# The last difference and low parts of x on VectorE instead of GpSimd, and part of w_out's preparation moved into the last stage

## The chip, the cores and the metric

The kernel runs on one core of a Trainium2 chip. The metric is the device time of one execution in microseconds (us); the time of a kernel is the median of its runs. Engines are called TensorE (PE in the profile; PEld is its loading of weights), VectorE (DVE), ScalarE (ACT), GpSimd (POOL) and SyncE (SP, which only issues DMAs here).

## What is computed

The reference is a chain of three parts in float32:

- attention within chunks of 64 tokens: 8 batches, 8 heads, 576 tokens, head size 64; softmax of q k^T / 8 and the product with v. Its output is a matrix x of 4608 tokens by 512;
- a mixture of 8 experts with capacity 576: the pairs of token and expert are taken in order of falling logit, so that each token gets one expert and each expert 576 tokens; each token's row then goes through relu(x @ w1[e]) @ w2[e], with 1024 hidden values;
- a last feed-forward part:

```python
def _moe2_ref(x, w1, w2, w3, w_out):
    h = np.maximum(np.maximum(x @ w1, x @ w2), x @ w3)   # 512 -> 768
    return (h @ w_out).astype(np.float32)                # 768 -> 512
```

## The kernel before, in words

Attention, routing and the experts come first (to about 656 us of the span). Products are made from float32 numbers that are split into a high part, which TensorE reads as float32r, and a low part, the rest. A split is two operations: ScalarE makes the high part by a cast, then another engine subtracts it from the number, which gives the low part.

The **last stage** is the third part of the reference. It runs over 6 blocks of 768 tokens (`for s in range(NS)`, line 1353). A 2x2 block product is done with seven products (a scheme of Strassen's kind): x of a block comes as four quarters b11, b12, b21, b22, and sums of them are needed, t1 = b12 - b11, t2 = b22 - t1, t3 = b22 - b12, t4 = b21 - t2. `xsum` (line 1070) makes one of these differences, `xsplit` (line 1077) splits one operand into high and low. Unsplit t1 and t4 share one place in the tile `hm`, t2 and t3 the other.

In a block, k runs over nine groups of columns of w1, w2 and w3. Each group has seven products, `p1` to `p7` (lines 1250 to 1281), of six matmuls each (line 1215). `p1` writes the PSUM bank px from b11, and ScalarE copies px to a row of the tile `tmp` (line 1254, its U1). `p6` writes py from t2, and VectorE adds U1 to it (line 1260, U2). `p2` accumulates b21's product onto the same px, so it has to follow the copy. `p5` (t1) writes pz, and `p7` (t3) accumulates onto py, so it has to follow line 1260. `p4` (t4) and `p3` (b22) belong to the group before: of the first group (k = 0) they come at k = 1. So k = 0 has the five products p1, p6, p2, p5, p7, in that order. Each product takes one of 8 tiles of weights (`ws`), and asks for the one 8 products on by a DMA on SP's queue (`wload`, line 1029).

When the nine groups of a block are done, h (unsplit in HR, split in HB) is multiplied with w_out for three sets of tokens, t = 3s, 3s + 1, 3s + 2: again seven products each (`o1` to `o7`, line 1294), with VectorE's sums `c22`, `c21`, `c12` (lines 1338 to 1351), and two scatters each of rows of the result by GpSimd (`scatter`, line 1304). Two sets are interleaved; then GpSimd drains (`pool.drain()`, line 1445) and the third set follows.

Between these products the kernel prepares the next block's x, where `more` is true (5 of the 6 blocks): t1, b11, t2, t4, b21 with VectorE's subtractions, and at the very end t3's difference and the low parts of t3, t4 and b22 with GpSimd's (lines 1456, 1460, 1461, 1469).

`wout(q, what)` (line 1036) prepares a third of w_out: "load" issues its DMAs, "sums" makes four differences on GpSimd, and `wout(q, range(...))` splits its seven operands, with ScalarE's casts (line 1063) and GpSimd's subtractions (line 1064). Thirds 1 and 2 are prepared in the first block of the last stage (lines 1376 to 1389). Third 0 is prepared in the last expert's second layer, `for d in range(4)` (lines 1177 to 1195), beside the preparation of the first block's x; its differences lie in `FP["u"]`, the tile whose first part is the `tmp` of the last stage.

The order of work on each engine is the order in which the program emits it (`tc.manual_schedule()`); an engine takes its instructions in that order, and the waits between engines come from the data. Nothing reorders the code around the change.

```python
    def xsplit(o, eng):
        nc.scalar.copy(XO[o][:, 0], xraw(o))
        eng.tensor_tensor(XO[o][:, 1], xraw(o), XO[o][:, 0].bitcast(F32), op=OP.subtract)
```

Of the kernel before, what the change touches and what calls it, by code (L numbers as in the profile page):

```python
# [7 lines left out]
F32 = mybir.dt.float32  # L8
# [691 lines left out]
def kernel(ctx, tc, q, k, v, w_gate, w1, w2, m1, m2, m3, m_out, out, mark=lambda n: None):  # L700
# [9 lines left out]
    rt = Router(ctx, tc, mark)  # L710
# [5 lines left out]
    P = rt.W = ctx.enter_context(tc.tile_pool(name="mw", bufs=1))  # L716
# [257 lines left out]

    split()
    XO, XR, WS, FP = {}, {}, [], {}
    HB, WQ, HR = {}, {}, {}
    USES = []
    for g in range(9 * NS):
        USES += [(g, 1), (g, 0)] + [(g - 1, 3), (g - 1, 6)] * (g % 9 > 0) + [(g, 2), (g, 4), (g, 5)]  # L980
# [2 lines left out]
    def homes():  # L983

        for o in ("b11", "t3", "b21", "b22", "t1", "t2", "t4"):
            XR[o] = ring.tile([128, 2048], F32R, name="x" + o, tag="chunk")
            XO[o] = XR[o][:, :4 * TB].rearrange("p (c a t) -> p c a t", c=2, a=2)
        W0 = [P.tile([128, 7, 256], F32R, name="wo%d" % i, tag=t) for i, t in enumerate(("c64", "pair"))]
        W1 = [ring.tile([128, 2048], F32R, name="wq%d" % i, tag="chunk")[:, :1792].rearrange("p (n f) -> p n f", n=7)
              for i in range(2)]  # L990
        WQ[0], WQ[1] = W0, W1
        for n, o in enumerate(("b11", "b21", "b22", "t1", "t2", "t3", "t4")):
            for x in range(2):
                WQ[0, n, x], WQ[1, n, x] = W0[x][:, n], W1[x][:, n]
                WQ[2, n, x] = XR[o][:, 4 * TB + 256 * x:4 * TB + 256 * x + 256]
        for i in range(2):
            t = P.tile([128, 4, 2, 2, 128], F32R, name="ws%d" % i, tag="raw%d" % i)
            WS.extend(t[:, j] for j in range(4))
        FP["u"] = P.tile([128, 5 * DM], F32, name="tmp", tag="xg")
        FP["m"] = ring.tile([128, 2048], F32, name="hm", tag="chunk")  # L1000
        FP["x"] = P.tile([128, 4 * TB], F32, name="xt", tag="aoh")

# [23 lines left out]
    def raw(x):  # L1026
        return x[:, 1].bitcast(F32)
# [8 lines left out]
    def wout(q, what):  # L1036

        mark("wout")
        lo = [WQ[q, n, 1].bitcast(F32) for n in range(7)]
        if what == "load":  # L1040
            top, low = mo[256 * q:256 * q + 128, :], mo[256 * q + 128:256 * q + 256, :]
            if q < 2:
                t = WQ[q][1].bitcast(F32)
                nc.sync.dma_start(t[:, 0:6:5], top.rearrange("p (c f) -> p c f", c=2))
                nc.sync.dma_start(t[:, 1:3], low.rearrange("p (c f) -> p c f", c=2))
            else:
                for n, (r, c) in ((0, (top, 0)), (5, (top, 256)), (1, (low, 0)), (2, (low, 256))):
                    nc.sync.dma_start(lo[n], r[:, c:c + 256])
        elif what == "sums":
            tq = WQ["t", q] = [FP["u"][:, 256 * i:256 * i + 256] if q == 0 else  # L1050
                               OT[2 * q - 2 + i // 2][:, i % 2 * 256:i % 2 * 256 + 256] for i in range(4)]
            for to, x, y in ((tq[0], lo[5], lo[0]), (tq[1], lo[2], tq[0]), (tq[3], lo[1], tq[1]), (tq[2], lo[2], lo[5])):
                nc.gpsimd.tensor_tensor(to, x, y, op=OP.subtract)
        else:
            jobs = [(WQ[q, n, 0], WQ[q, n, 1], lo[n] if n < 3 else WQ["t", q][n - 3]) for n in what]
            if q < 2 and what[0] == 0:
                jobs = [(WQ[q][0][:, 0:3], WQ[q][1][:, 0:3], WQ[q][1][:, 0:3].bitcast(F32))]
            elif q < 2:
                jobs = [(WQ[q][0][:, n:n + 2], WQ[q][1][:, n:n + 2],
                         (FP["u"][:, 256 * (n - 3):256 * (n - 1)] if q == 0 else OT[2 * q - 2 + (n - 3) // 2])  # L1060
                         .rearrange("p (n f) -> p n f", n=2)) for n in (3, 5)]
            for hi, to, x in jobs:
                nc.scalar.copy(hi, x)
                nc.gpsimd.tensor_tensor(to, x, hi.bitcast(F32), op=OP.subtract)
# [5 lines left out]
    def xsum(o, eng):  # L1070
        mark("ysplit")
        b12 = raw(XO["t3"])
        a, b = {"t1": (b12, xraw("b11")), "t2": (xraw("b22"), xraw("t1")), "t3": (xraw("b22"), b12),
                "t4": (xraw("b21"), xraw("t2"))}[o]
        eng.tensor_tensor(xraw(o), a, b, op=OP.subtract)

    def xsplit(o, eng):
        mark("ysplit")
        nc.scalar.copy(XO[o][:, 0], xraw(o))
        eng.tensor_tensor(XO[o][:, 1], xraw(o), XO[o][:, 0].bitcast(F32), op=OP.subtract)  # L1080
# [9 lines left out]
    for r in range(E):  # L1090
# [54 lines left out]
        if r + 1 == E:  # L1145
# [8 lines left out]
            dve, pool = nc.vector, nc.gpsimd  # L1154
        state["l1"] = False
        for d in range(4):
            have(8 * r + 4 + d + 1)
            w = [x.rearrange("p (a f) -> p a f", a=8) for x in chunks[8 * r + 4 + d]]
            acc = PS.tile([128, 2, 512], F32, name="acc")
            for hf in range(2):  # L1160
                tk = slice(hf * 288, hf * 288 + 288)
                n = 0
                for f in range(8):
                    mark("mm2")
                    for a, x in ((0, hh), (1, hh), (0, hl)):
                        nc.tensor.matmul(acc[:, hf, :288], w[a][:, f, :], x[:, f, tk], start=n == 0, stop=n == 23)  # L1166
                        n += 1
                    if n % 6 == 0 and n < 24:
                        pump()
                if hf == 1:  # L1170
                    mark("yev")
                    ys = P.tile([128, CAP], F32, name="ys", bufs=2)
                    nc.scalar.copy(ys.rearrange("p (a t) -> p a t", a=2), acc[:, :, :288])  # L1173
                    nc.scalar.dma_start(yd[d * 128:d * 128 + 128, r * CAP:(r + 1) * CAP], ys)
                    state["used"] += 1
                pump()
            if r + 1 == E:
                if d == 0:
                    xsum("t1", dve)
                    xsplit("b11", dve)  # L1180
                    xsum("t2", dve)
                    xsplit("t1", dve)
                elif d == 1:
                    xsum("t4", dve)
                    xsplit("t2", dve)
                    xsplit("b21", dve)
                    wout(0, "sums")
                elif d == 2:
                    xsum("t3", dve)
                    xsplit("t3", dve)  # L1190
                    xsplit("t4", dve)
                    wout(0, range(3))
                else:
                    xsplit("b22", dve)
                    wout(0, range(3, 7))


    c3.close()
# [1 line left out]
    blocks()  # L1200
    TMP = FP["u"][:, :5 * TB].rearrange("p (n t) -> p n t", n=5)
    OT = [P.tile([128, 512], F32, name="ot", tag="ys", bufs=2) for _ in range(2)]
    OT += [P.tile([128, 512], F32, name="ot2", tag="ct"), rt.C.tile([128, 512], F32, name="ot3", tag="i32")]
    XB, YZ, U = {}, {}, {}
    tt = dve.tensor_tensor
    scat = []
# [146 lines left out]
    for s in range(NS):  # L1353
        for k in range(9):
            g, q = 9 * s + k, (k - 1) // 3
            p1(g)
            p6(g)
            if k:
                p4(g - 1)
                if k % 3 == 0:  # L1360
                    hsum(q, dve, "s1", "s2", "s3")
                    high(q, "s1", "s3", "s2")
                    low(q, pool, "s1")
                p3(g - 1)
                if k % 3 == 0:
                    hsum(q, pool, "s4")
                    high(q, "a12", "s4")
                    low(q, pool, "s3", "a12", "s2", "a22", "a11", "s4")
            p2(g)
            if k % 3 == 2:  # L1370
                high(k // 3, "a22")
            p5(g)
            p7(g)
            if k % 3 == 2:
                high(k // 3, "a11")
            if s == 0:
                if k == 0:
                    wout(1, "load")
                elif k == 1:
                    wout(1, "sums")  # L1380
                    wout(1, range(3))
                elif k == 2:
                    wout(1, range(3, 7))
                    wout(2, "load")
                elif k == 4:
                    wout(2, "sums")
                    wout(2, range(3))
                elif k == 5:
                    wout(2, range(3, 7))
        more = s + 1 < NS  # L1390
        t = 3 * s
# [61 lines left out]
        o7(t)  # L1453
        if more:
            xsplit("b21", dve)
            xsum("t3", pool)
        o5(t)
        c22(t)
        if more:
            xsplit("t3", pool)  # L1460
            xsplit("t4", pool)
        o4(t)
        c21(t)
        scatter(t, 0)
# [1 line left out]
        c12(t)  # L1466
        scatter(t, 1)
        if more:
            xsplit("b22", pool)


# [25 lines left out]
```

## Time and profile before

| | |
|---|---|
| median of 3 runs | 1212.24 us (1211.3 to 1213.85) |
| profiled execution, its own time | 1212.45 us |
| its span, first to last instruction | 1210.6 us |
| mean granted TensorE clock | 0.984 |
| TensorE busy | 1166.8 us (96%) |
| TensorE loading weights | 1112.2 us (92%) |
| VectorE busy | 852.8 us (70%) |
| GpSimd busy | 490.6 us (41%) |
| ScalarE busy | 432.2 us (36%) |
| chain that ended last | TensorE 86%, VectorE 4%, issue 3%, ScalarE 2%, GpSimd 2%, others 3% or less together |

All times in the trace count from the start of the span; the time of an execution has a little more than the span. Busy times are of the engines' own work; issuing a DMA does not count on SP. The ends of matmuls are modelled, so that one group of matmuls seems to overlap the next. The granted clock is a share of TensorE's full speed of 2.4 GHz. In a timeline a row is: start in us, duration in us, engine, line, operation, output and inputs, number of instructions merged into it, and in brackets how long the engine was idle before it and which instruction's end released it. The chain goes back from the last instruction, at each step to what released it.

### The profile page before, as it was taken

What the parts mean: (1) busy time and instruction counts of PE and PEld (TensorE: products, weight loads), DVE (VectorE), ACT (ScalarE), POOL (GpSimd) and SP (SyncE); (2) the same over time, 40 slices, a digit from 0 to 9 for tenths busy, and PEclk for the clock granted to TensorE, in tenths of its full rate; (3) what the DMA queues carried; (4) which work ended last, traced back from release to release, by engine and by line L of the source; (5) the groups of instructions that cost most, each with busy time, mean ns of one, the idle gap of its engine ahead of it and who ended that gap; (6) DMA issues with size and microseconds to landing.
All of it is one profiled execution on the core that took longest, in us unless ns stands there. A gap on an engine that the chain in (4) does not pass through costs nothing.

```text
span 1210.6 us, 25836 instructions
## 1 busy us (share of the span) xinstructions
PE 1166.8 (96%) x9994; PEld 1112.2 (92%) x9994; DVE 852.8 (70%) x1745; ACT 432.2 (36%) x738; POOL 490.6 (41%) x660
## 2 busy tenths in 40 slices
PE   7999979999999999999999998999999999999998
PEld 6788857999999999999999998999999999999997
DVE  6888976788788888888733665566566566566564
ACT  5888822243333333325313223123223223223221
POOL 8432201011027564757863554333333333333332
PEclk8999978999999999999999999999999999999999
DMA  9999615273646556568663983884884884884871
GB/s 263 259 256 267 170 45 166 89 238 123 204 146 221 173 193 216 185 210 271 209 209 127 285 253 111 249 253 149 254 253 148 252 254 147 254 253 146 257 222 53
DMA packets 229962, 243.16 MB, mean 201 GB/s; under 512 B 34640, under 2 KB 209744, under 8 KB 229840
## 3 DMA queue, kind: packets, MB, share of 16 engines
q1 hardware_dynamic: 209728, 180.92, 49.9%
q0 software_dynamic: 14976, 51.13, 12.7%
q10 hardware_dynamic: 5136, 9.46, 2.2%
q8 instruction: 80, 1.31, 0.5%
q14 instruction: 42, 0.34, 0.1%
HBM read 195.05 MB, written 46.40 MB: 199 GB/s over the span
## 4 chain that ended last, share of the span: by engine, by line
PE 86%; DVE 4%; issue 3%; ACT 2%; POOL 2%; SPq 1%; DMA 1%; POOLq 0%; ACTq 0%; DVEq 0%
PE acc L1166 17%; PE acc L1112 16%; PE py L1215 14%; PE pz L1215 9%; PE px L1215 9%; PE pX L181 3%; PE px L1294 2%; PE pT L115 2%; PE py L1294 2%; PE pS L132 2%; PE pA L168 2%; PE po L1294 2%; PE pxt L821 1%; PE pY L199 1%; PE pz L1294 1%
## 5 line engine op out<-in xcount | busy, mean ns | idle before, releaser
L1166 PE MATMUL acc<-hhi,chunk 128*128 128x288 f32 x1024 | 209.9, 299 | 0.0
L1112 PE MATMUL acc<-xhi,chunk 128*128 128x288 f32 (+2 forms) x1024 | 206.5, 300 | 2.7 <-DVE chunk L768 1.3
L1215 PE MATMUL py<-xt,ws 128*128 128x384 f32 x972 | 188.1, 335 | 0.0
L1215 PEld LDWEIGHTS py<-xt,ws 128*128 128x128 f32 x972 | 170.6, 189 | 0.6 <-DVE tmp L1280 0.6
L1112 PEld LDWEIGHTS acc<-xhi,chunk 128*128 128x128 f32 x1024 | 160.7, 188 | 4.1 <-DVE hlo L1143 1.6
L1166 PEld LDWEIGHTS acc<-hhi,chunk 128*128 128x128 f32 x1024 | 162.9, 188 | 0.3
L1166 PE MATMUL acc<-hlo,chunk 128*128 128x288 f32 x512 | 150.8, 294 | 0.0
L1215 PE MATMUL px<-xb,ws 128*128 128x384 f32 x648 | 131.6, 337 | 12.7 <-ACT tmp L1254 12.0
L1112 PE MATMUL acc<-xlo,chunk 128*128 128x288 f32 (+2 forms) x512 | 143.1, 295 | 0.0
L1215 PEld LDWEIGHTS px<-xb,ws 128*128 128x128 f32 x648 | 114.0, 189 | 15.0 <-ACT tmp L1254 13.9
L798 POOL DMA_INDIRECT xg<-xd,idx x40 | 43.1, 1077 | 168.4 <-DVE ohe L688 89.8
L1166 PEld LDWEIGHTS acc<-hlo,chunk 128*128 128x128 f32 x512 | 96.1, 188 | 0.0
L1112 PEld LDWEIGHTS acc<-xlo,chunk 128*128 128x128 f32 x512 | 93.4, 188 | 0.0
L1134 ACT ACTIVATE hhi<-acc 128x576 fp32r<-128x576 f32 (+1 forms) x66 | 41.9, 638 | 136.4 <-PE acc L1112 133.7
L768 DVE TENSOR_TENSOR chunk<-raw,chunk 128x1024 fp32r<-128x1024 f32 x64 | 80.6, 1265 | 5.7 <-ACT chunk L761 5.6
L1280 DVE TENSOR_TENSOR tmp<-py,tmp 128x384 f32<-128x384 f32 x54 | 30.1, 557 | 72.7 <-PE py L1215 72.6
L1260 DVE TENSOR_TENSOR tmp<-py,tmp 128x384 f32<-128x384 f32 x54 | 30.1, 558 | 64.3 <-ACT tmp L1254 48.9
L1143 DVE SCALAR_TENSOR_TENSOR hlo<-acc,hhi 128x576 fp32r<-128x576 f32 (+1 forms) x66 | 48.3, 736 | 30.7 <-ACT hhi L1134 30.4
L761 ACT CAST chunk<-raw 128x1024 fp32r<-128x1024 f32 x64 | 66.6, 1047 | 8.0 <-ACT ys L1173 6.4
L1254 ACT COPY tmp<-px 128x384 f32<-128x384 f32 x54 | 25.8, 479 | 119.4 <-PE px L1215 118.3
L1215 PE MATMUL pz<-xt,ws 128*128 128x384 f32 x324 | 65.8, 338 | 0.0
L1215 PE MATMUL pz<-xb,ws 128*128 128x384 f32 x324 | 64.8, 334 | 0.0
(326 smaller groups left out, 2412.5 us busy)
## 6 DMA issues: line engine op xcount, KB each, us to landing
ws<-wdb SPq DMA_DIRECT2D x216, 256.0 KB
ws<-wda SPq DMA_DIRECT2D x162, 256.0 KB
raw<-in_moe_w_dram SPq DMA_DIRECT2D x64, 512.0 KB
xd<-x POOLq DMA_DIRECT2D x36, 256.0 KB, 4.1
yd<-ys ACTq DMA_DIRECT2D x32, 288.0 KB
wdb<-pair POOLq DMA_DIRECT2D x18, 512.0 KB, 5.3
ink<-in_k_dram SPq DMA_DIRECT2D x16, 512.0 KB
inq<-in_q_dram SPq DMA_DIRECT2D x16, 512.0 KB
```

Of the source, the lines that this page charges most:

```text
L181: nc.tensor.matmul(PX[g][c * 64:(c + 1) * 64, hp, :], AT[g][:, hp, c * 64:c * 64 + 64], VB[u % 3][:, 2 * h + c, hp].rearrange("p s i -> p ...
L761: nc.scalar.copy(hi, raw)
L768: nc.vector.tensor_tensor(lo, raw, hi.bitcast(F32), op=OP.subtract)
L798: nc.gpsimd.indirect_dma_start(out=g, out_offset=None, in_=xd[:, :], in_offset=bass.IndirectOffsetOnAxis(ap=rt.idx[r][:, t:t + 1], axis=0))
L1112: nc.tensor.matmul(acc[:, hf, :tk.stop - tk.start], w[a][:, dc, o:o + 128], x[:, dc, tk], start=n == 0, stop=n == 11)
L1134: nc.scalar.activation(hv, src, AF.Relu)
L1143: nc.vector.scalar_tensor_tensor(lv, src, 0.0, hv.bitcast(F32), op0=OP.max, op1=OP.subtract)
L1166: nc.tensor.matmul(acc[:, hf, :288], w[a][:, f, :], x[:, f, tk], start=n == 0, stop=n == 23)
L1215: nc.tensor.matmul(dst, w[:, dc, a], XO[x][:, c, dc], start=start and n == 0, stop=stop and n == 5, skip_group_check=True)
L1260: tt(U[g, 2], YZ[g][0], U[g, 1], op=OP.add)
L1280: tt(u3, YZ[g][0], U[g, 1], op=OP.add)
L1294: nc.tensor.matmul(bank(t, i), HB[q, o][x][:, t % 3 * 128:t % 3 * 128 + 128], WQ[q, n, a], start=start and q == qs[0] and m == 0, stop=sto ...
```

## The change

Three things change:

- at the end of each block but the last, t3's difference and the low parts of t3, t4 and b22 go from GpSimd to VectorE. The difference and the split of t3 stand behind `c22` of the third set of tokens, the splits of t4 and b22 behind `c12` and the last scatter;
- in the last expert's second layer the splits of third 0 of w_out are taken out; b22's split moves from the fourth chunk (d = 3) to the third, ahead of t4's. The splits of third 0 are emitted in the first block of the last stage at k = 0, behind `p7` and ahead of the loads of third 1;
- the differences of third 0 go to the two tiles `ot2` and `ot3` instead of to `FP["u"]`. These tiles are now made earlier; later they hold third 2's differences and results, as before.

```diff
--- before.py
+++ after.py
@@ -974,7 +974,7 @@
 
     split()
     XO, XR, WS, FP = {}, {}, [], {}
-    HB, WQ, HR = {}, {}, {}
+    HB, WQ, HR, O2 = {}, {}, {}, []
     USES = []
     for g in range(9 * NS):
         USES += [(g, 1), (g, 0)] + [(g - 1, 3), (g - 1, 6)] * (g % 9 > 0) + [(g, 2), (g, 4), (g, 5)]
@@ -997,6 +997,7 @@
             t = P.tile([128, 4, 2, 2, 128], F32R, name="ws%d" % i, tag="raw%d" % i)
             WS.extend(t[:, j] for j in range(4))
         FP["u"] = P.tile([128, 5 * DM], F32, name="tmp", tag="xg")
+        O2.extend((P.tile([128, 512], F32, name="ot2", tag="ct"), rt.C.tile([128, 512], F32, name="ot3", tag="i32")))
         FP["m"] = ring.tile([128, 2048], F32, name="hm", tag="chunk")
         FP["x"] = P.tile([128, 4 * TB], F32, name="xt", tag="aoh")
 
@@ -1047,8 +1048,7 @@
                 for n, (r, c) in ((0, (top, 0)), (5, (top, 256)), (1, (low, 0)), (2, (low, 256))):
                     nc.sync.dma_start(lo[n], r[:, c:c + 256])
         elif what == "sums":
-            tq = WQ["t", q] = [FP["u"][:, 256 * i:256 * i + 256] if q == 0 else
-                               OT[2 * q - 2 + i // 2][:, i % 2 * 256:i % 2 * 256 + 256] for i in range(4)]
+            tq = WQ["t", q] = [(OT if q == 1 else O2)[i // 2][:, i % 2 * 256:i % 2 * 256 + 256] for i in range(4)]
             for to, x, y in ((tq[0], lo[5], lo[0]), (tq[1], lo[2], tq[0]), (tq[3], lo[1], tq[1]), (tq[2], lo[2], lo[5])):
                 nc.gpsimd.tensor_tensor(to, x, y, op=OP.subtract)
         else:
@@ -1057,8 +1057,7 @@
                 jobs = [(WQ[q][0][:, 0:3], WQ[q][1][:, 0:3], WQ[q][1][:, 0:3].bitcast(F32))]
             elif q < 2:
                 jobs = [(WQ[q][0][:, n:n + 2], WQ[q][1][:, n:n + 2],
-                         (FP["u"][:, 256 * (n - 3):256 * (n - 1)] if q == 0 else OT[2 * q - 2 + (n - 3) // 2])
-                         .rearrange("p (n f) -> p n f", n=2)) for n in (3, 5)]
+                         (OT if q == 1 else O2)[(n - 3) // 2].rearrange("p (n f) -> p n f", n=2)) for n in (3, 5)]
             for hi, to, x in jobs:
                 nc.scalar.copy(hi, x)
                 nc.gpsimd.tensor_tensor(to, x, hi.bitcast(F32), op=OP.subtract)
@@ -1188,11 +1187,8 @@
                 elif d == 2:
                     xsum("t3", dve)
                     xsplit("t3", dve)
+                    xsplit("b22", dve)
                     xsplit("t4", dve)
-                    wout(0, range(3))
-                else:
-                    xsplit("b22", dve)
-                    wout(0, range(3, 7))
 
 
     c3.close()
@@ -1200,7 +1196,7 @@
     blocks()
     TMP = FP["u"][:, :5 * TB].rearrange("p (n t) -> p n t", n=5)
     OT = [P.tile([128, 512], F32, name="ot", tag="ys", bufs=2) for _ in range(2)]
-    OT += [P.tile([128, 512], F32, name="ot2", tag="ct"), rt.C.tile([128, 512], F32, name="ot3", tag="i32")]
+    OT += O2
     XB, YZ, U = {}, {}, {}
     tt = dve.tensor_tensor
     scat = []
@@ -1375,6 +1371,8 @@
                 high(k // 3, "a11")
             if s == 0:
                 if k == 0:
+                    wout(0, range(3))
+                    wout(0, range(3, 7))
                     wout(1, "load")
                 elif k == 1:
                     wout(1, "sums")
@@ -1453,12 +1451,11 @@
         o7(t)
         if more:
             xsplit("b21", dve)
-            xsum("t3", pool)
         o5(t)
         c22(t)
         if more:
-            xsplit("t3", pool)
-            xsplit("t4", pool)
+            xsum("t3", dve)
+            xsplit("t3", dve)
         o4(t)
         c21(t)
         scatter(t, 0)
@@ -1466,7 +1463,8 @@
         c12(t)
         scatter(t, 1)
         if more:
-            xsplit("b22", pool)
+            xsplit("t4", dve)
+            xsplit("b22", dve)
 
 
 # ---- launch: one core; inputs and outputs as the reference has them ----
```

## Rows read from the trace of the kernel before

**Rows 1.** Waits of TensorE from 653 us on: total us, times, longest.

```profile
PE px L1215 <- ACT tmp L1254: 12.0, 6, 3.8
PE px L1215 <- ACT ys L1173: 0.7, 1, 0.7
```

**Rows 2.** Timeline of TensorE at the second block boundary (columns as described above).

```profile
842.66 1.21 PE L1215 MATMUL px<-xb,ws 128*128 128x384 f32 x6
...
846.49 1.31 PE L1215 MATMUL px<-xb,ws 128*128 128x384 f32 x6 [1.58 <-ACT tmp L1254]
...
849.72 1.20 PE L1215 MATMUL px<-xb,ws 128*128 128x384 f32 x6
...
850.76 2.24 PE L1215 MATMUL py<-xt,ws 128*128 128x384 f32 x12
```

**Rows 3.** Timeline of TensorE at the first block boundary.

```profile
747.42 1.21 PE L1215 MATMUL px<-xb,ws 128*128 128x384 f32 x6
...
753.49 2.29 PE L1215 MATMUL px<-xb,ws 128*128 128x384 f32 x6 [3.82 <-ACT tmp L1254]
...
759.21 1.23 PE L1215 MATMUL px<-xb,ws 128*128 128x384 f32 x6
```

**Rows 4.** Windows at the first boundary: us, engines' busy time, PEclk, DMA share, GB/s.

```profile
753.00:756.00 3.00, 2.51 (x8) 2.52 (x9) 0.56 (x1) 0.57 (x3) 2.85 (x4) 0.50 0.00 0
760.00:764.00 4.00, 4.00 (x25) 4.00 (x24) 2.08 (x4) 0.48 (x1) 0.00 (x0) 1.00 0.74 227
```

**Rows 5.** Timelines of TensorE, GpSimd and ScalarE at the start of the last stage.

```profile
656.22 1.31 PE L1215 MATMUL px<-xb,ws 128*128 128x384 f32 x6 [0.73 <-ACT ys L1173]
...
657.99 2.76 POOL L1064 TENSOR_TENSOR wo<-tmp,wo 128x512 fp32r<-128x512 f32 x2 [3.39 <-ACT wo L1063]
...
659.55 0.48 ACT L1254 COPY tmp<-px 128x384 f32<-128x384 f32 x1 [1.10 <-POOL wo L1064]
...
660.08 1.31 PE L1215 MATMUL px<-xb,ws 128*128 128x384 f32 x6 [1.50 <-ACT tmp L1254]
```

**Rows 6.** Timelines of GpSimd, VectorE and ScalarE at the second block boundary.

```profile
838.40 1.32 POOL L1309 DMA_INDIRECT out_dram<-ot,ia  x1 [0.22 <-issue]
...
838.79 0.95 DVE L1080 TENSOR_TENSOR xt<-hm,xt 128x768 fp32r<-128x768 f32 x1
...
840.00 0.95 DVE L1080 TENSOR_TENSOR xb<-xb 128x768 fp32r<-128x768 f32 x1
...
840.87 0.42 DVE L1339 TENSOR_TENSOR ot<-pz,tmp 128x256 f32<-128x256 f32 x1
...
841.89 1.83 POOL L1075 TENSOR_TENSOR hm<-xb,xt 128x768 f32<-128x768 f32 x1 [2.17 <-PE py L1294]
...
843.76 1.57 ACT L1079 CAST xt<-hm 128x768 fp32r<-128x768 f32 x2 [3.98 <-POOL hm L1075]
...
845.23 0.83 ACT L1079 CAST xb<-xb 128x768 fp32r<-128x768 f32 x1
...
845.97 0.47 ACT L1254 COPY tmp<-px 128x384 f32<-128x384 f32 x1
...
846.47 0.56 DVE L1260 TENSOR_TENSOR tmp<-py,tmp 128x384 f32<-128x384 f32 x1 [3.18 <-ACT tmp L1254]
```

**Rows 7.** Instructions of line 1075 on VectorE: count, ns min/median/max, first and last start.

```profile
L1075 DVE TENSOR_TENSOR hm<-xb,hm x10: 947/948/950, 738.5 to 1109.7; 128x768 f32<-128x768 f32 x10
```

**Rows 8.** Instructions of lines 1063 and 1064 for third 0 of w_out.

```profile
L1063 ACT CAST wo<-tmp x2: 613/618/622, 657.3 to 657.8; 128x512 fp32r<-128x512 f32 x2
...
L1063 ACT CAST wo<-wo x1: 832/832/832, 651.7 to 651.7; 128x768 fp32r<-128x768 f32 x1
...
L1064 POOL TENSOR_TENSOR wo<-tmp,wo x2: 1272/1396/1519, 658.0 to 659.5; 128x512 fp32r<-128x512 f32 x2
...
L1064 POOL TENSOR_TENSOR wo<-wo,wo x1: 1952/1952/1952, 652.7 to 652.7; 128x768 fp32r<-128x768 f32 x1
```

**Rows 9.** Timeline of VectorE in the last expert, beside GpSimd's differences.

```profile
645.60 1.49 DVE L1080 TENSOR_TENSOR xb<-xb 128x768 fp32r<-128x768 f32 x1
```

## The prediction

> **What bounds the kernel now.** By the table of the profile the chain that ended last is TensorE for 86% of the span, so the first view to read is what TensorE itself waited for in the last stage, from 653 us to the end. It shows one kind of wait: 12.0 us in six pieces, all for the same release, the ScalarE copy of px at line 1254 (line 1294's matmuls, the block's results, show none) [rows 1]. That copy is `p1`'s, and `p2`, which accumulates into the same px, may not start before it is done. The other 0.7 us is the change of stages and is not touched.
>
> The second view is TensorE's timeline where a block ends and the next begins. In steady state one product follows the other at 1.04 us (849.72 to 850.76). The five products of k = 0 should thus take 5.20 us, from `p1` of one group to `p1` of the next; at the second boundary they take 849.72 - 842.66 = 7.06 us [rows 2]. The loss is 1.86 us: 1.58 us idle and some 0.27 us of refilling behind it (the first matmul after the wait has a group of 1.31 instead of 1.20 us). At the first boundary the same five take 759.21 - 747.42 = 11.79 us, a loss of 6.59 [rows 3]; the idle time there is 3.82 us, and behind it the granted clock stands at 0.50, the level of 1.2 GHz, and at 1.00 again from 760 us [rows 4]. Idle time and refill are 4.09 of the 6.59, so the low clock costs 2.50 us. The third to fifth boundary repeat the second, and the stage's start does too, with 1.50 us idle [rows 5]. In all: 12.0 + 6 x 0.27 + 2.50 = 16.1 us. More than this the change cannot give back, since it touches no other wait of TensorE.
>
> The third view says why the copy is late: the timelines of the other engines at the second boundary [rows 6]. GpSimd ends the issue of a scatter at 839.72 and starts the sum for t3 at 841.89; between them stands the drain of line 1445, which GpSimd must finish first. The sum takes 1.83 us. ScalarE, which works in order, waits for it until 843.76, casts t3, t4 and b22 (two in 1.57 us, then 0.83), and only then makes the copy of px, 845.97 to 846.44, although px was complete near 843.87. VectorE is idle meanwhile.
>
> **The change, part by part.**
>
> *t3's sum and the three subtractions move to VectorE.* The work on TensorE and ScalarE is the same. Per boundary GpSimd loses a sum of 1.83 us and three subtractions, and VectorE gains four operations of 0.95 us [rows 7]. I lay them out at the second boundary, letting an operation start 0.08 us before its predecessor ends, as the one of 840.00 with 0.95 us is followed at 840.87 [rows 6]. `c22` runs 840.87 to 841.29; t3's sum 841.21 to 842.16; ScalarE's cast of t3 842.20 to 843.03, t4's from 842.94, b22's 843.68 to 844.51 (0.74 apart, like 845.23 and 845.97); the copy of px 844.42 to 844.89. `p2` can start at 844.94, against 842.66 + 2 x 1.04 = 844.74 without any wait. So 0.20 us of wait stays, with 0.11 of refill: 0.3 us per boundary instead of 1.86. An idle time of 0.2 us is far under the 1.58 us behind which the second boundary kept the full rate of 1.04 us, so I take the first boundary's low clock as gone too; at most its 2.50 us stays.
>
> What is late next is VectorE. `c21` and `c12` now stand behind t3's subtraction, which waits for ScalarE's cast: t3's low part 843.05 to 844.00, `c21` from 843.92, `c12` from 844.26, t4's low part 844.60 to 845.55, b22's 845.47 to 846.42, and then line 1260's sum of py, 0.56 us, until 846.90. `p7` writes that py and would start at 844.94 + 1.15 + 1.04 = 847.13. The slack is 0.2 us, so this costs nothing if each operation keeps its length; every 0.1 us beyond it is paid at five boundaries. `p7` needs t3's low part (844.00), `p4` and `p3` need those of t4 and b22 a group later. The banks that `c21` and `c12` free are wanted two products or more later: nothing. On GpSimd the two scatters wait behind them for `c21` and `c12` as before, with no sum or subtraction in the way: nothing either, nobody waits for their end inside the block. The SP queue holds only weight and block loads, in their old order.
>
> *wout(0) moves into the first group of the last stage, and its differences go to two other tiles.* At the start TensorE's `p2` waits until 660.08 for the copy of px, because that copy goes into the tile in which wout(0)'s differences lie; ScalarE had to wait until GpSimd had read them, 1.10 us, behind two casts [rows 5]. With the other tiles and with casts emitted later, ScalarE is free after its last result copy and b22's cast goes a chunk earlier. `p1` ends near 657.53, the copy ends 0.48 later at 658.01, `p2` could start at 658.30: no wait is left. The 1.50 + 0.27 us are gained whole. What moves: casts of 0.83 + 2 x 0.62 us on ScalarE, subtractions of 1.95 + 2 x 1.40 us on GpSimd [rows 8]. The casts come after `p2`'s copy, near 660.2, and end near 662.2, before the next `p1` (661.4 to 662.6) wants its copy; GpSimd is then idle until wout(1)'s differences, whose data are loaded in the same place as before. No DMA is issued by the moved part. So it costs nothing; without that cover one 0.5 us wait.
>
> A price that the trace shows only from far is VectorE beside GpSimd. A subtraction of 0.95 us took 1.49 us while GpSimd ran a difference [rows 9]; the one at 838.79 kept 0.95 us beside a scatter's issue (838.40, 1.32 us) [rows 6]. The new low parts meet scatters only, which the second row resembles, so I take 0.95; the other end is +0.54 for each of the two that run beside scatters.
> The Trainium skill (SBUF — State Buffer, section "Who interferes with whom") says that a VectorE instruction with two SBUF inputs contends with a GpSimd instruction that reads SBUF, and that the one that starts first blocks the other wholly; if the scatter counts as such a reader, VectorE would wait out each one. The trace agrees for the difference and, by the operation at 838.79, not for the scatter.
>
> **Sum.** 16.1 - 5 x 0.3 = 14.6 us off the profiled execution's 1212.45 us (span 1210.6): 1197.85. The median of the runs, 1212.24, lies 0.2 lower: 1197.6.
>
> **Rivals.**
> *A, VectorE becomes the bound at the boundary.* If t4's and b22's low parts are stretched by 0.54 us each, `p7` waits 1.08 - 0.2 = 0.9 us, five times 4.4: 1202. If each waits out a whole scatter of up to 1.32 us, it is 2.4 us, five times 12: 1209.6. For it: a slack of only 0.2 us. Against: the operation at 838.79. The skill's page named above is the strict form of this. Chance 0.12.
> *B, the sum for t3 waits for more than GpSimd's drain.* The trace puts GpSimd's idle time before it down to a matmul [rows 6]; if that is a true need, VectorE's sum starts at 841.89 and not 841.21, 0.7 us later, and at the first boundary still nearly 3 us late. Then 4 x 0.7 + 2.9 = 5.7 us are missing: 1203. Against: the program orders this sum only behind operations of VectorE. Chance 0.09.
> *C, slower: VectorE is locked for the whole of GpSimd's scatters and drain*, in the stretch from `c22` to line 1260's sum, so that TensorE idles at `p7` as long as at the first boundary today and falls to the lower clock each time. That costs 6.59 us at each of five boundaries, 33.0, against 14.4 lost there now and 1.8 gained at the start: 1229. It decides from 3.2 us per boundary on (16.1 / 5). Against it speaks the same 0.95 us beside a scatter. Chance 0.04.
> *D, the wait is only renamed:* `p2` waits for something else that ends as late, and the time stays at 1212. For it only that one releaser is named per wait. Chance 0.03.
>
> **Numbers.** Forecast 0.72. A measurement of this kernel tells a difference from no change beyond about 0.2%, 2.4 us. Forecast, A and B are faster: 0.93; D the same: 0.03; C slower: 0.04. The lower end is the whole 16.1 us with the spread of the runs (1211.3 is 0.9 under the median): 1195.0. The upper end takes in B and the milder A with a spread: 1203.5; the strict A, C and D are left out.
>
> **What would show it.** TensorE's waits for line 1254: six of 12.0 us should be five of about 0.2 us or none; granted clock 1.00 at 750 to 760; t3's sum on VectorE directly behind `c22`, and ScalarE's three casts behind it without a gap; VectorE's low parts at 0.95 us; no wait of TensorE for line 1260 above 0.2 us; no wait at the stage's start. It is wrong if the boundary's five products still take 6 us or more, whichever release is then named.

## The result and the profile after

The changed kernel takes 1197.48 us (median of 6 runs, 1195.41 to 1200.57), the kernel before, over 6 runs, 1212.59 us: a ratio of 0.9878, with a 95% interval of 0.9851 to 0.9904. The profiled execution took 1197.39 us with a span of 1195.6. Its line numbers in the last stage are one to four lower than before: the copy of px is line 1250, the sum of py line 1256, the products line 1211.

What TensorE waited for from 640 us on, in the view of the waits (total, times, longest):

```profile
PE px L1211 <- ACT ys L1172: 0.7, 1, 0.7
PE px L1211 <- ACT tmp L1250: 0.2, 1, 0.2
```

The 12.0 us of [rows 1] are 0.2. (This view gives idle time alone, and the ends of matmuls are modelled; what is still lost beside it shows in the times of the products.) The timeline of TensorE at the stage's start, the first and the second boundary (the first and third `px` row of each are `p1` of two groups, the middle one is `p2`):

```profile
655.16 1.33 PE L1211 MATMUL px<-xb,ws 128*128 128x384 f32 x6 [0.73 <-ACT ys L1172]
...
657.37 1.20 PE L1211 MATMUL px<-xb,ws 128*128 128x384 f32 x6
...
660.49 1.20 PE L1211 MATMUL px<-xb,ws 128*128 128x384 f32 x6
...
745.05 1.21 PE L1211 MATMUL px<-xb,ws 128*128 128x384 f32 x6
...
747.46 1.32 PE L1211 MATMUL px<-xb,ws 128*128 128x384 f32 x6 [0.15 <-ACT tmp L1250]
...
750.70 1.20 PE L1211 MATMUL px<-xb,ws 128*128 128x384 f32 x6
...
834.11 1.21 PE L1211 MATMUL px<-xb,ws 128*128 128x384 f32 x6
...
836.37 1.31 PE L1211 MATMUL px<-xb,ws 128*128 128x384 f32 x6
...
839.60 1.20 PE L1211 MATMUL px<-xb,ws 128*128 128x384 f32 x6
```

The five products take 5.33, 5.65 and 5.49 us where they took 7.09, 11.79 and 7.06 [rows 2, 3, 5]; without any loss it would be 5.20. The clock no longer falls at the first boundary, where it is 1.00 from 755 to 760 us too; the windows there (busy time of PE, PEld, DVE, ACT, POOL, then PEclk, DMA share, GB/s) answer to [rows 4]:

```profile
745.00:750.00 5.00, 4.84 (x28) 4.53 (x28) 3.83 (x6) 2.88 (x5) 2.71 (x4) 1.00 0.33 103
750.00:755.00 5.00, 5.00 (x30) 5.00 (x30) 2.23 (x4) 0.48 (x1) 0.20 (x1) 1.00 0.95 317
```

The timelines of VectorE, ScalarE and GpSimd at the second boundary answer to [rows 6]:

```profile
832.32 0.42 DVE L1335 TENSOR_TENSOR ot<-pz,tmp 128x256 f32<-128x256 f32 x1
832.65 0.95 DVE L1074 TENSOR_TENSOR hm<-xb,xt 128x768 f32<-128x768 f32 x1
...
833.63 1.57 ACT L1078 CAST xt<-hm 128x768 fp32r<-128x768 f32 x2 [2.39 <-DVE hm L1074]
...
834.50 0.96 DVE L1079 TENSOR_TENSOR xt<-hm,xt 128x768 fp32r<-128x768 f32 x1 [0.90 <-ACT xt L1078]
...
835.11 0.83 ACT L1078 CAST xb<-xb 128x768 fp32r<-128x768 f32 x1
835.85 0.47 ACT L1250 COPY tmp<-px 128x384 f32<-128x384 f32 x1
...
836.04 0.95 DVE L1079 TENSOR_TENSOR xt<-hm,xt 128x768 fp32r<-128x768 f32 x1
836.08 1.76 POOL L1305 DMA_INDIRECT out_dram<-ot,ia  x1 [2.76 <-DVE ot L1341]
...
836.91 0.95 DVE L1079 TENSOR_TENSOR xb<-xb 128x768 fp32r<-128x768 f32 x1
...
837.78 0.55 DVE L1256 TENSOR_TENSOR tmp<-py,tmp 128x384 f32<-128x384 f32 x1
...
838.14 0.97 POOL L1305 DMA_INDIRECT out_dram<-ot,ia  x1 [0.21 <-issue]
```

t3's difference (832.65) stands directly behind `c22`, ScalarE's three casts follow it without a gap, and the copy of px ends at 836.32, 2.2 us after `p1` began, against 3.8 before.

Executions differ by several us ahead of the last stage: in the profiles below it starts anywhere from 651.6 to 659.0 us. So beside the time each run is read by its **stage length**, the span minus the start of the first `p1`: 554.38 us before, 540.44 after, 13.94 less.

### The profile page after: what moved, and what is told of

Same layout as the page of the kernel before. It is cut to its first block, busy times and chain, and to the rows that moved or that the text cites. A ratio compares the mean times of both kernels' runs of the same rounds, so it can differ in the third digit from the quotient of the medians.

```text
span 1195.6 us, 25800 instructions
## 1 busy us (share of the span) xinstructions
PE 1163.4 (97%) x9994; PEld 1108.2 (93%) x9994; DVE 866.1 (72%) x1765; ACT 432.0 (36%) x738; POOL 461.6 (39%) x640
## 4 chain that ended last, share of the span: by engine, by line
PE 88%; DVE 4%; DMA 3%; SPq 1%; ACT 1%; issue 1%; another core or an unknown queue 1%; POOL 0%; POOLq 0%; ACTq 0%; DVEq 0%
PE acc L1111 16%; PE acc L1165 16%; PE py L1211 14%; PE pz L1211 9%; PE px L1211 9%; PE px L1290 3%; PE py L1290 3%; PE po L1290 3%; PE pX L181 3%; DMA vb<-in_v_dram 2%; PE pz L1290 2%; PE pT L115 2%; PE pS L132 2%; PE pA L168 1%; PE pxt L821 1%; PE pY L199 1%
## 5 line engine op out<-in xcount | busy, mean ns | idle before, releaser
L1305 POOL DMA_INDIRECT out_dram<-ot,ia x36 | 44.6, 1240 | 56.7 <-DVE ot L1341 51.1
```

Of the source, the lines that this page charges most:

```text
L1305: st = pool.indirect_dma_start(out=out, out_offset=bass.IndirectOffsetOnAxis(ap=ia[:, col:col + 1], axis=0), in_=ot, in_offset=None)
```

## The experiments

**Each part alone.** First the boundary alone, on the kernel before (lines 1456 to 1469 as in the change, nothing of w_out's part).

> The kernel before with t3's difference and the three low parts on VectorE, and nothing of w_out's part. Theory (two separate waits of TensorE for the same kind of copy): every boundary as in the changed kernel, five products of k = 0 in 5.5 to 5.65 us, and the stage's start as before, 7.1 us with 1.5 us idle; 1197.5 + 1.8 = 1199.3 us. Rival (the parts need each other, for instance through GpSimd's queue): boundaries of 6 us or more, above 1202 us.

Measured 1199.17 us, ratio to the kernel before on the same chip (as in all that follows) 0.9898 (0.9863 to 0.9933). The boundaries take 5.49 to 5.51 us, the stage's start 7.09, stage length 541.41. TensorE's waits keep one piece of the six:

```profile
PE px L1215 <- ACT tmp L1254: 1.5, 1, 1.5
```

Then w_out's part alone: the changed kernel with the old end of the block.

```diff
             xsplit("b21", dve)
+            xsum("t3", pool)
...
-            xsum("t3", dve)
-            xsplit("t3", dve)
+            xsplit("t3", pool)
+            xsplit("t4", pool)
...
-            xsplit("t4", dve)
-            xsplit("b22", dve)
+            xsplit("b22", pool)
```

> The changed kernel with the boundary's four operations back on GpSimd. Theory: only the stage's start gains, 5.3 us for its five products instead of 7.1; the first boundary stays at 11.8 us with the granted clock at 0.50, the others at 7.1 to 7.35; 1212.5 - 1.8 = 1210.8 us. Rival (w_out's part helps GpSimd at the first boundary too): the first boundary under 10 us, below 1209 us.

Measured 1211.46 us against 1210.49, ratio 1.0004 (0.9977 to 1.0030): the times do not tell this part from no change, and a gain of 1.8 us lies within their interval. The trace shows the gain: the start takes 5.31 us, the stage 551.71, and of six waits five are left. The later boundaries stay at 7.05 to 7.35; the first takes 10.81, where the low clock cost 0.9 us less than in the profile before.

```profile
PE px L1211 <- ACT tmp L1250: 10.4, 5, 3.8
```

So each part removes its own waits and leaves the other's, and in the trace their sizes are those expected: the five boundaries take 27.5 us with the first part alone and 27.6 in the changed kernel, the start 5.31 with the second alone and 5.33.

**Which half of w_out's part?** The kernel before with only the other tiles; the splits stay in the last expert.

```diff
-            tq = WQ["t", q] = [FP["u"][:, 256 * i:256 * i + 256] if q == 0 else
-                               OT[2 * q - 2 + i // 2][:, i % 2 * 256:i % 2 * 256 + 256] for i in range(4)]
+            tq = WQ["t", q] = [(OT if q == 1 else O2)[i // 2][:, i % 2 * 256:i % 2 * 256 + 256] for i in range(4)]
...
```

> The kernel before with only the other tiles for the differences of third 0 of w_out; their splits stay in the last expert. Theory (the shared tile made the copy of px wait for GpSimd): the copy follows ScalarE's casts at once, from 658.4 to 658.9 on the clock of the kernel before, so that TensorE idles 0.4 to 0.5 us instead of 1.5: the first five products in 5.8 to 6.0 us instead of 7.1. Rival (the order of the casts alone): 7.1 us as before.

Measured in a single execution, 1205.72 us; the start takes 5.88 us, with 0.29 us idle. By this one profile the shared tile made 1.2 of the 1.8 us, and the rest is ScalarE's casts ahead of the copy, which here end at 653.86 us, 0.9 after px is complete.

**Which of the four moved operations matter?** The changed kernel with only the difference on VectorE.

```diff
-            xsplit("t3", dve)
+            xsplit("t3", pool)
+            xsplit("t4", pool)
...
-            xsplit("t4", dve)
-            xsplit("b22", dve)
+            xsplit("b22", pool)
```

> The changed kernel with only t3's difference on VectorE; the low parts of t3, t4 and b22 back on GpSimd in their old places. Theory (the casts of ScalarE wait for the difference alone, and the low parts have room): boundaries at 5.5 us, the first perhaps 0.5 more because GpSimd's drain lies ahead of t3's low part there; 1197.5 us, at most 1198.5. Rival (GpSimd's slow low parts cost too): boundaries of 6 us or more, or a new wait of p7, p4 or p3; 1201 us or more.

Measured 1197.94 us, ratio 0.9884 (0.9848 to 0.9920), stage 540.35: the same as the change. All boundaries take 5.49 to 5.51 us. The only cost of GpSimd's low parts is at the first boundary, where b22's comes 0.4 us late for `p3`:

```profile
PE pz L1211 <- POOL xb L1079: 0.4, 1, 0.4
```

So the gain of the boundaries' five products is the difference's alone. Moving the three low parts gave nothing that the times can show; in the trace it spares the wait for `p3` behind the first boundary, 0.7 us with the refilling.

**Drain or slow engine?** The difference may have been late because GpSimd had to drain first, or because it needs 1.83 us for it. The kernel before, without line 1445:

```diff
         scatter(t + 1, 1)
-        pool.drain()
```

> The kernel before without GpSimd's drain, all else as it was. Theory (the drain makes the sum late, not GpSimd's 1.83 us): at the second boundary the sum starts at the end of the last scatter's issue, 2.1 us earlier, at the first 4.4 us earlier; the copy of px ends before p2 wants it; boundaries of 5.2 to 5.5 us, 1212.5 - 12.7 = 1199.8 us. Rival (GpSimd's speed): boundaries of 6.5 us or more, 1206 us or more.

The boundaries take 5.20 to 5.21 us, as the theory of the drain has it, though this run alone does not decide that: behind the new wait told of below `p1` itself comes 1.4 us later, which gives ScalarE that much more time. And the time is 1207.48 us, ratio 0.9973 (0.9955 to 0.9991), far from 1199.8. The stage length is 550.01, 4.4 less than before. The five boundaries give 14.4 us (40.4 to 26.0), but 6.9 are lost to a new wait ahead of each boundary, with the refilling behind it, and 3.2 at the end. The waits of TensorE, and the timelines of VectorE, GpSimd and TensorE ahead of the second boundary:

```profile
PE pz L1294 <- DVE ot L1339: 5.6, 5, 1.1
```

```profile
831.92 1.84 POOL L1075 TENSOR_TENSOR hm<-xb,xt 128x768 f32<-128x768 f32 x1
...
832.10 2.48 DVE L1080 TENSOR_TENSOR xb<-xb 128x768 fp32r<-128x768 f32 x1
...
834.50 0.41 DVE L1339 TENSOR_TENSOR ot<-pz,tmp 128x256 f32<-128x256 f32 x1
...
834.97 0.61 PE L1294 MATMUL pz<-wo,hbhlo 128*128 128x256 f32 x3 [1.12 <-DVE ot L1339]
```

Without the drain the difference runs on GpSimd from 831.92 to 833.76, and b21's low part, which VectorE starts 0.18 us later, takes 2.48 us instead of 0.95: it ends 0.82 us after GpSimd's operation. `c22` behind it is late, and `o3` on TensorE waits 1.12 us for `c22`, in each of five blocks (5.6 us). Blocks two to five grow outside the boundary from 83.4 to 84.8 us. And the end grew: from TensorE's last matmul to the end of the span it is 9.0 us instead of 5.8.

With the drain kept, but behind the difference:

```diff
         scatter(t + 1, 1)
-        pool.drain()
...
             xsum("t3", pool)
+        pool.drain()
```

> The kernel before with the drain directly behind t3's difference on GpSimd instead of ahead of it. Theory of the drain: the four later boundaries at 5.2 to 5.5 us, as t3's low part still ends before p7 wants it; at the first boundary the drain's 4.3 us now lie ahead of t3's low part, and p7 may wait up to 1 us for it: 5.5 to 6.5 us; 1199.8 to 1201 us. Rival (GpSimd's speed): as in the kernel before, 1206 us or more.

Measured 1204.63 us, ratio 0.9950 (0.9928 to 0.9971), stage 547.35, boundaries 5.21: the end is as before, the wait for `c22` stays at 5.6 us. My guess for the first boundary was wrong in place: the drain still held GpSimd for 3.52 us there, but t3's low part came in time for `p7`, and b22's was 0.3 us late for `p3`.

```profile
745.99 1.83 POOL L1075 TENSOR_TENSOR hm<-xb,xt 128x768 f32<-128x768 f32 x1
...
751.35 3.64 POOL L1080 TENSOR_TENSOR xt<-hm,xt 128x768 fp32r<-128x768 f32 x2 [3.52 <-PE pz L1294]
```

Now the collision can be taken away: against the run before, b21's split goes behind `c22`.

```diff
         if more:
-            xsplit("b21", dve)
             xsum("t3", pool)
         pool.drain()
         o5(t)
         c22(t)
         if more:
+            xsplit("b21", dve)
             xsplit("t3", pool)
```

> The kernel before with the drain behind t3's difference on GpSimd, as in the run before it of that name, and with b21's split moved behind c22, so that no VectorE operation with two inputs in SBUF meets that difference ahead of c22. Theory (b21's low part is blocked for the whole of GpSimd's difference, 2.48 us instead of 0.95, and makes c22 late for o3; c22, with one input in PSUM, is not blocked): the wait of 1.1 us for c22 is gone in all five blocks, later blocks of 88.6 us from first product to first product instead of 90.0, the last stage 540.4 us instead of 547.4, the time 6.9 us lower, 1197.7. Rival (anything on VectorE is slowed beside GpSimd, or c22 was late for another reason): c22 itself takes over 0.6 us, the wait stays at 0.8 us or more, no gain over 1204.6 us.

```profile
835.28 1.83 POOL L1075 TENSOR_TENSOR hm<-xb,xt 128x768 f32<-128x768 f32 x1
...
836.18 0.42 DVE L1339 TENSOR_TENSOR ot<-pz,tmp 128x256 f32<-128x256 f32 x1 [0.64 <-PE pz L1294]
836.52 1.42 DVE L1080 TENSOR_TENSOR xb<-xb 128x768 fp32r<-128x768 f32 x1
...
838.11 1.21 PE L1215 MATMUL px<-xb,ws 128*128 128x384 f32 x6
...
840.20 1.20 PE L1215 MATMUL px<-xb,ws 128*128 128x384 f32 x6
...
843.32 1.20 PE L1215 MATMUL px<-xb,ws 128*128 128x384 f32 x6
```

`c22` (836.18), in the middle of GpSimd's difference, keeps 0.42 us; b21's low part, started when 0.6 us of the difference were left, takes 1.42. The wait for `c22` is gone, the third to fifth blocks take 88.61 to 88.62 us from first product to first product, and the time is 1200.77 us on a chip where the kernel before takes 1213.68, ratio 0.9893 (0.9869 to 0.9916). The boundaries take 5.21 us (843.32 - 838.11), the first 5.24, now with no wait that would make `p1` late. The stage length is 542.15, not 540.4: at the first boundary `p3` now waits 1.6 us for b22's low part on GpSimd, behind the drain. So the drain made the difference late. A difference on GpSimd ahead of the drain gains nearly as much as one on VectorE (541.41 with the boundary's part alone), but here only since nothing that TensorE soon waits for meets it on VectorE.

**How much room has VectorE?** The changed kernel with t4's subtraction made a second time behind b22's:

```diff
             xsplit("b22", dve)
+            dve.tensor_tensor(XO["t4"][:, 1], xraw("t4"), XO["t4"][:, 0].bitcast(F32), op=OP.subtract)
```

> The changed kernel with t4's subtraction made twice on VectorE at each boundary, the second time behind b22's: one more operation of 0.95 us (0.87 with the overlap) ahead of the sum that p7 waits for. Theory (VectorE has 0.2 us of room or less there): the sum ends 0.87 us later, p7 waits 0.7 to 0.85 us, with 0.1 us of refill: five boundaries of 6.2 to 6.4 us, 1197.5 + 4.2 = 1201.7 us. Rival (VectorE is not near the bound): boundaries unchanged, 1197.5 us.

```profile
PE py L1211 <- DVE tmp L1256: 2.5, 5, 0.5
```

`p7` waits at all five boundaries, and they take 6.29 to 6.32 us, 0.8 more than in the change: 0.70 us later start of `p7` and 0.1 of refill. Of the 0.87 us, then, 0.17 were room. The stage is 3.45 us longer than the change's. The time, 1199.30 us with a ratio of 0.9901 (0.9882 to 0.9920), lies 2.4 under what was expected, but on this chip the kernel before takes 1210.81 and not 1212.59; the expected 1201.7 is 0.991 of the latter, which lies within the interval.

**What is left at a boundary?** The changed kernel with the splits of t4 and b22 in the next block.

```diff
-            xsplit("t4", dve)
-            xsplit("b22", dve)
...
             p6(g)
+            if s and k == 0:
+                xsplit("t4", dve)
...
             p5(g)
+            if s and k == 0:
+                xsplit("b22", dve)
             p7(g)
```

> The changed kernel with the splits of t4 and b22 moved behind the next block's p6 and p5, so that ScalarE's copy of px stands directly behind t3's cast. Theory (the 0.3 us left per boundary are ScalarE's casts ahead of the copy): boundaries of 5.2 us and no wait of TensorE there, five times 0.3 = 1.5 us less: 1196.0 us. Rival (the rest comes from elsewhere, or t4's and b22's low parts are late for p4 and p3): boundaries at 5.5 us, or a new wait at k = 1; 1197.5 us or more.

Measured 1194.39 us, ratio 0.9870 (0.9849 to 0.9892), with boundaries of 5.20 to 5.21 us, a stage of 538.20 and no wait of TensorE left but the change of stages:

```profile
PE px L1211 <- ACT ys L1172: 0.7, 1, 0.7
```

The five boundaries give 5 x 0.3 = 1.5 of the 2.24 us by which the stage is shorter than the change's; the rest lies in the first block and the end, which vary by some 0.5 us. The intervals of the two ratios overlap, so the times alone do not part this version from the change; the stage and the waits do. It has the lowest ratio and the shortest stage of all versions run.

## Why the prediction was right

- *What bounds.* TensorE's waits for the copy of px and what they bring with them, refilling and the low clock, were the whole matter. The losses against 5.20 us, from 1.89 + 6.59 + 1.86 + 2.15 + 1.93 + 1.88 = 16.3 us to 0.13 + 0.45 + 0.29 + 0.29 + 0.32 + 0.28 = 1.8, fell by 14.5; the sum said 14.6. The stage fell by 13.94: 0.45 of the rest is in the first block outside these products, 0.18 in the last.
- *How much of the hit is luck.* The mechanism and its size are right, by the losses. That the median, 1197.48, comes as near as 0.1 to the forecast's 1197.6 is chance: the runs of the changed kernel spread from 1195.41 to 1200.57. The profiled execution is 15.06 us shorter, 13.94 of them in the last stage; the other 1.1 lie ahead of it, where executions of one and the same code differ by more.
- *The drain as the cause.* Shown by the runs with the drain later, and most plainly by the one in which `c22` is not late either: the boundary then takes 5.21 us with GpSimd's slow difference. Rival B, a wait for more than the drain, falls with that, and with the difference at 832.65 in the profile after.
- *The residue of 0.3 us.* 0.29 at the second boundary, and the run with late casts shows that it is ScalarE's casts ahead of the copy. The first boundary keeps 0.45: there VectorE stood idle for 0.46 us ahead of `o7`'s sum, and everything behind it came later. No other profile shows that, and its cause is open.
- *The low clock.* Gone with the idle time behind which it came; the granted clock is 1.00 in both windows. It is gone in the run with the boundary's part alone too, where the first boundary takes 5.50 us.
- *Room of 0.2 us on VectorE.* 0.17 by the run with one operation more. Rival A did not come in, since the low parts beside the scatters kept 0.95 us (836.04 and 836.91); I took the row at 838.79 of [rows 6] for it and not [rows 9], and that decided between 1197.6 and 1202. What the two scatters do is now also plain from the other side: the one at 836.08 took 1.76 us where an undisturbed one (838.14) takes 0.97.
- *w_out's part.* 1.76 of 1.77 us. That its splits cost nothing in the first group holds: `p2` starts 2.21 us after `p1`, with the casts behind it.
- Rivals C and D did not come in: no boundary takes over 5.65 us, and no wait of another name appears.
- One reading was loose: VectorE is not idle all the while GpSimd makes the difference in the kernel before; it does `c21` and `c12`, 0.4 us each, which changes no term.
- Of the moved operations I gave the three low parts no gain and no cost; the run with the difference alone bears that out but for the 0.7 us behind the first boundary.

Where I was wrong was behind the prediction: I expected 1199.8 us without the drain, and counted only the wait that goes. The difference on GpSimd is then early enough to meet b21's low part on VectorE. It is the price of [rows 9], at a place where I had not looked for it.

## What to carry to other kernels

Follow a wait of the bound engine back through every engine in its chain: here ScalarE's copy was late because of a cast, the cast because of one difference, and the difference because of an order of GpSimd's queue (a drain) that had nothing to do with it. Move the one operation that ends last; here the three beside it could have stayed. Before an operation is made to start earlier on GpSimd, look at what VectorE does in that stretch, and for how long somebody can wait for VectorE.

## What the runs showed of the hardware

- A VectorE subtraction with both inputs in SBUF that starts during a GpSimd operation of the same kind is held nearly to the end of it: it took 2.48 us and ended 0.82 past the other's end, and 1.42 us when 0.6 of the other were left, against 0.95 alone. A VectorE sum with one input in PSUM, started during such an operation, kept its 0.42 us. The Trainium skill (SBUF — State Buffer, section "Who interferes with whom") states both: two SBUF inputs contend with a GpSimd instruction that reads SBUF and the second to start is blocked wholly; with at most one, outside the 2-port modes, it does not contend. The trace agrees, but for 0.13 us: waiting out the whole difference and then taking 0.95 us would make 2.61.
- Beside the issue of a scatter the same subtraction lost nothing, but the issue took 1.76 us instead of 0.97 where the subtraction began just ahead of it, and 1.32 us at 838.40 of [rows 6].
- In the kernel before and in the changed one GpSimd's next instruction behind the drain came 2.1 to 2.5 us after the last scatter's issue at most boundaries and 4.3 to 4.4 at the first; without a drain there it came after 0.1 us. Why the first is longer was not settled. Without any drain the end of the kernel, behind the last matmul, was 3.2 us longer; what the last drain saves there was not tried apart.
